# A gated mix of two spectral filters on one core: the order of the first loads, two sums done in halves, rows of half the spectrum, and the last block

## The chip, the core and the metric

One core of a Trainium2 chip runs the whole kernel as one program. The metric is the device time of one execution in microseconds (us); lower is better. Five engines work side by side, each through its own instructions in order: TensorE (matmuls, PE in the profile; the loads of its stationary operand are the rows PEld), VectorE (DVE), ScalarE (ACT), GpSimd (POOL) and SyncE (SP), which here only issues DMA transfers. They wait for each other through semaphores.

## The reference

```python
def _ref(x, w_r, w_i):                       # the same for A and for B
    X = jnp.fft.rfft2(x.astype(jnp.float32), axes=(-2, -1))      # x: 1 x 2048 x 1024
    X = X * (w_r + 1j * w_i)                                      # w: 2048 x 513
    return jnp.fft.irfft2(X, s=(S, D), axes=(-2, -1)).astype(jnp.bfloat16)

x = A_x
g = sigmoid((x * gate_w).sum(-1, keepdims=True))
out = g * _ref(x, A_w_r, A_w_i) + (1 - g) * _ref(x, B_w_r, B_w_i)
```

Both filters act on the same x. So there is one forward transform, two products with weights, and one inverse transform into which the gate is folded.

## The kernel before

The transforms are matmuls with constant tables, in stages. A unit of work fills two of the eight banks of the matmuls' accumulators (PSUM, 1024 columns of float32); there are four such units, and most matmul outputs are copied out by ScalarE, some by VectorE (`act_copy`, `dve_copy`, lines 325 and 328).

- Stage 1 (`stage1`, lines 440 and 447): the first part of the transform over the 2048 rows. x comes in eight blocks `c` of four row groups, 512 KB each; each block is worked for two sets of 128 columns, `j`. `prep` (lines 419 and 423) writes a mirrored copy of the block, or, for the blocks in `FOLDED`, sum and difference, which halve the matmul columns. `mvariant` (lines 412 and 414) scales the table M into three more forms. `evict1` writes the tile FT.
- Stage 2 (`stage2`, line 476) does the transform over the 1024 columns as a sum over `j`, stage 4 (`stage4`, line 491) the rest of the rows. The work is split in two sets of frequencies, M and O, of eight pieces each; two pieces form a group q, four groups to a set. `evict4` leaves a group's spectra in a slot of the tile XR; three slots serve "direct" groups, two serve swapped ones. `swap` (POOL) makes a copy of a group with real and imaginary partitions exchanged by two DMAs.
- Products (`product`, line 521, VectorE): D with the direct spectra, S with the swapped ones, each in two halves of 128 columns; D writes the tile WB, S the tile WA. The weights W lie in WA too: set M needs columns 0 to 384 of a row (`("W", "M", q)`), set O a further 128 (`("W", "O", b)`), which are loaded over columns of M that have been used by then, from 258 on.
- Gate: `gate_weights` (POOL reverses a row at line 526, TensorE multiplies at 528), `gate_spectrum` (line 535), `row_sums` (VectorE, lines 554 and 555, with the table VC), `star_column` and `star_products` (one column of the spectrum, with W's column 256), later `gate_diag`, `zsum`, `sigma`, `gate_sign`.
- Stage 5 (`stage5`, line 575): the inverse over part of the rows, 32 groups g of eight frequencies; groups from 16 up need all products of set M, the others all of set O. `edge` (line 653) forms two columns by themselves for group 0. `evict5` writes the tile WB.
- Stages 6 and 7 (`stage6`, line 675; `stage7`, line 688): for each of 16 blocks r the rest of the inverse. `evict6` and `odd_copy` bring results out, `finals` (line 701, VectorE) adds and subtracts, and SP stores the block. `rbgen` makes the gated tables for stage 6.

The order on each engine is written out by hand in the text `PLAN`: a token is name, arguments, unit, engine (`s2.M.1.1.pe` is stage 2, set M, piece 1, unit 1 on TensorE; `a` is ScalarE, `d` VectorE). An engine's instructions are the tokens for it, from left to right. `Prog` derives the waits from what each instruction reads and writes. Loads are issued in the order of the code ahead of the plan: SP's queue holds x with M's pieces, then F2 and a first part of CK, then W of set M in four groups, two further parts of CK (KI and CL) and, by the plan, W of set O and the tables U5 and DI. Twelve matmuls on zeros (line 375) run while the first loads are under way.

Of the kernel before, what the change touches and what calls it, by code (L numbers as in the profile page):

```python
# [10 lines left out]
HA, HB = 258, 264  # L11
# [139 lines left out]
mv.0.2..d mv.0.1..d mv.0.3..d pp.0..d s1.0.0.0.pe mv.1.1..a mv.2.1..d mv.3.1..d mv.2.3..a mv.2.2..d s1.0.1.1.pe  # L151
e1.0.0..a pp.1..d e1.0.1..a gw.2.pe s1.1.0.3.pe pp.2..d egw..a s1.1.1.0.pe e1.1.0..a s1.2.0.1.pe e1.1.1..d
mv.7.1..a s1.2.1.2.pe mv.4.2..a pp.3..d mv.4.1..a mv.4.3..a e1.2.1..a mv.5.1..d s1.3.1.3.pe pp.4..d e1.2.0..a
mv.6.3..d s1.4.1.0.pe mv.6.2..d mv.7.3..d mv.6.1..d e1.3.1..a s1.3.0.2.pe pp.5..d s1.4.0.1.pe e1.3.0..a pp.6..d
s1.5.0.3.pe e1.4.0..a mv.7.2..d s1.6.0.2.pe e1.4.1..d e1.5.0..a s1.6.1.1.pe pp.7..d e1.6.0..a s1.7.0.0.pe
e1.6.1..d s1.5.1.3.pe e1.7.0..a s1.7.1.2.pe e1.5.1..d e1.7.1..a s2.M.1.1.pe s2.M.0.0.pe e2.M.1..a s2.M.2.3.pe
e2.M.0..a s4.M.1.2.pe e2.M.2..a s4.M.0.1.pe e4.M.1..a s4.M.2.0.pe e4.M.0..a gs.3.3.pe e4.M.2..a D.M.0.0..d
sw.M.0..dma s2.M.3.2.pe egs.3..a D.M.0.1..d s2.M.4.1.pe e2.M.3..a gs.1.0.pe e2.M.4..a s4.M.3.3.pe egs.1..a
s4.M.4.2.pe e4.M.3..a s2.M.5.1.pe e4.M.4..a D.M.1.0..d sw.M.1..dma gs.0.0.pe e2.M.5..a S.M.0.1..d s2.M.7.3.pe
egs.0..a s4.M.5.2.pe S.M.0.0..d e2.M.7..a gs.2.1.pe e4.M.5..a D.M.1.1..d s4.M.7.0.pe egs.2..a sw.M.2..dma  # L160
rows..d s2.M.6.3.pe e4.M.7..a s2.O.1.2.pe e2.M.6..a S.M.1.1..d s2.O.0.1.pe e2.O.1..a D.M.2.0..d s4.M.6.0.pe
e2.O.0..a S.M.1.0..d s4.O.1.3.pe e4.M.6..a wo.0..spq s4.O.0.2.pe D.M.2.1..d e4.O.1..a sw.M.3..dma s2.O.3.1.pe
e4.O.0..a S.M.2.0..d s2.O.2.0.pe e2.O.3..a S.M.2.1..d s2.O.7.3.pe e2.O.2..a D.M.3.0..d s4.O.3.2.pe sw.O.0..dma
e2.O.7..a s4.O.2.1.pe D.M.3.1..d e4.O.3..a s2.O.6.0.pe e4.O.2..a D.O.0.0..d s4.O.7.3.pe e2.O.6..a S.M.3.0..d
s2.O.5.2.pe e4.O.7..a s4.O.6.1.pe S.M.3.1..d e2.O.5..a st.0.pe s2.O.4.3.pe D.O.1.0..d sw.O.1..dma wo.1..spq
e4.O.6..a s5.16.2.pe e2.O.4..a dz.1..d dz.0..d s5.19.1.pe e5.16..a D.O.0.1..d s5.24.3.pe est..a e5.19..a
D.O.3.0..d s4.O.4.2.pe e5.24..a S.O.0.1..d s4.O.5.0.pe e4.O.4..a s5.20.1.pe S.O.0.0..d e4.O.5..a s5.25.3.pe
e5.20..a stp..d sw.O.2..dma D.O.1.1..d s5.17.2.pe e5.25..a s5.23.0.pe S.O.1.0..d e5.17..a s5.21.1.pe D.O.3.1..d
e5.23..a s5.18.3.pe e5.21..a S.O.1.1..d s5.27.2.pe e5.18..a D.O.2.1..d sw.O.3..dma zs.0.0.pe e5.27..a
s5.26.1.pe D.O.2.0..d s5.30.3.pe S.O.2.1..d e5.26..a s5.22.2.pe e5.30..a S.O.2.0..d U5..dma s5.31.1.pe e5.22..a  # L170
# [94 lines left out]
def bass_gated_mix__spectral_gfnet__spectral_gfnet__prompt_kernel(nc, A_x, A_w_r, A_w_i, B_x, B_w_r, B_w_i, gate_w, out):  # L265
# [20 lines left out]
    ATB = sb("ATB", 32)  # L286
    XST = sb("XST", 64)
# [60 lines left out]
    FOLDED = (1, 3, 5)  # L348


    MP = ((0, 4), (4, 16), (16, 32))
# [503 lines left out]
```

## Time and profile before

| What | us |
| --- | --- |
| time, median of 3 runs (lowest to highest) | 128.36 (128.15 to 129.1) |
| the profiled execution's own time | 128.09 |
| its span, first to last instruction | 126.2 |
| stage 1's first matmul / stage 2's first matmul | 7.85 / 23.49 |
| first matmul of stage 5 / its end, by the chain | 53.34 / 91.79 |
| first matmul of stage 6 / last store issued | 92.87 / 123.73 |

| Engine | busy us | share of the span |
| --- | --- | --- |
| PE | 114.4 | 91% |
| PEld | 98.9 | 78% |
| ACT | 103.7 | 82% |
| DVE | 88.4 | 70% |
| POOL | 14.2 | 11% |

Times inside the execution count from the start of the span. In the table by windows, each row is a stretch of the span: its length, then each engine's busy time with the count of its instructions, TensorE's granted clock, the DMA engines' share and their GB/s. In a timeline a row is: start, length, engine, line, operation, output and input, shapes, count; the bracket gives the idle time before it and what ended it. "q" behind an engine's name is its instruction queue, where DMA transfers are issued. In the chain of work that ended last, a row is start, length and what the end waited for there. Matmuls are pipelined: a 128-column matmul is shown 219 ns long but the next starts 56 ns later, so costs of TensorE are taken from start to start.

### The profile page before, as it was taken

What the parts mean: (1) busy time and instruction counts of PE and PEld (TensorE: products, weight loads), DVE (VectorE), ACT (ScalarE), POOL (GpSimd) and SP (SyncE); (2) the same over time, 40 slices, a digit from 0 to 9 for tenths busy, and PEclk for the clock granted to TensorE, in tenths of its full rate; (3) what the DMA queues carried; (4) which work ended last, traced back from release to release, by engine and by line L of the source; (5) the groups of instructions that cost most, each with busy time, mean ns of one, the idle gap of its engine ahead of it and who ended that gap; (6) DMA issues with size and microseconds to landing.
All of it is one profiled execution on the core that took longest, in us unless ns stands there. A gap on an engine that the chain in (4) does not pass through costs nothing.

```text
span 126.2 us, 3590 instructions
## 1 busy us (share of the span) xinstructions
PE 114.4 (91%) x1538; PEld 98.9 (78%) x1538; DVE 88.4 (70%) x120; ACT 103.7 (82%) x124; POOL 14.2 (11%) x31
## 2 busy tenths in 40 slices
PE   6957789699999999999999999999969999999950
PEld 2246569579688695797999989999969999999920
DVE  0075997206198999999999989994001977787782
ACT  0448999598888999999998996998969788988850
POOL 5800000003023033041303000000000000000000
PEclk9999999999999999999999999999999999999999
DMA  2999999999999999979744596000000243443344
GB/s 49 298 346 343 348 374 337 255 272 284 336 303 352 359 322 311 215 192 208 151 166 166 140 405 291 8 0 5 0 0 5 100 173 143 169 168 140 121 160 166
DMA packets 26832, 25.81 MB, mean 205 GB/s; under 512 B 10241, under 2 KB 22801, under 8 KB 26561
## 3 DMA queue, kind: packets, MB, share of 16 engines
q1 hardware_dynamic: 24144, 20.11, 52.3%
q0 software_dynamic: 1584, 4.43, 9.7%
q10 hardware_dynamic: 1088, 1.05, 2.5%
q8 instruction: 12, 0.20, 0.7%
q14 instruction: 4, 0.02, 0.1%
HBM read 17.19 MB, written 4.19 MB: 169 GB/s over the span
## 4 chain that ended last, share of the span: by engine, by line
PE 44%; DVE 23%; DMA 11%; ACT 11%; issue 5%; SPq 3%; DVEq 1%
PE PS L675 11%; DVE WB L521 11%; PE PS L688 11%; DVE WA L521 10%; PE PS L575 10%; DMA XR<-c_M 7%; DMA XR<-XR 5%; ACT FT L325 4%; PE PS L476 4%; ACT WB L325 4%; PE PS L447 3%; PE PS L491 3%; SPq L322 3%; ACT XR L412 1%; ACT WA L325 1%
## 5 line engine op out<-in xcount | busy, mean ns | idle before, releaser
L575 PE MATMUL PS<-CK,WA 128*128 128x128 bf16 x256 | 34.0, 232 | 0.4 <-DVE WA L521 0.3
L575 PEld LDWEIGHTS PS<-CK,WA 128*128 128x128 bf16 x256 | 33.4, 153 | 0.8 <-DVE WA L521 0.6
L575 PE MATMUL PS<-CK,WB 128*128 128x128 bf16 x256 | 33.9, 225 | 0.0
L575 PEld LDWEIGHTS PS<-CK,WB 128*128 128x128 bf16 x256 | 33.5, 153 | 0.4 <-ACT WB L325 0.2
L325 ACT ACTIVATE WB<-PS 128x1024 bf16<-128x1024 f32 (+1 forms) x31 | 31.2, 1022 | 2.3 <-PE PS L575 1.5
L325 ACT ACTIVATE XR<-PS 128x1024 bf16<-128x1024 f32 x32 | 30.0, 1050 | 3.0 <-PE PS L476 2.0
L701 DVE TENSOR_TENSOR WA<-PS,WA 128x512 bf16<-128x512 f32 x32 | 21.4, 725 | 15.8 <-ACT WA L325 15.8
L325 ACT ACTIVATE WA<-PS 128x1024 bf16<-128x1024 f32 (+2 forms) x33 | 25.2, 820 | 5.0 <-PE PS L675 4.8
L521 DVE TENSOR_TENSOR WB<-XR,WA 128x2048 bf16<-128x2048 bf16 x16 | 19.1, 1222 | 9.2 <-PE PS L535 6.6
L521 DVE TENSOR_TENSOR WA<-XR,WA 128x2048 bf16<-128x2048 bf16 x16 | 19.0, 1223 | 0.3 <-DMA XR<-XR 0.3
L476 PE MATMUL PS<-F,FT 128*128 128x128 bf16 x256 | 15.8, 219 | 1.1 <-ACT FT L325 1.1
L688 PE MATMUL PS<-FT,WA 128*128 128x256 bf16 x128 | 16.4, 273 | 0.2 <-ACT WA L325 0.2
L476 PEld LDWEIGHTS PS<-F,FT 128*128 128x128 bf16 x256 | 14.7, 98 | 2.4 <-ACT FT L325 1.4
L491 PE MATMUL PS<-XR,CK 128*128 128x512 bf16 (+1 forms) x72 | 15.3, 355 | 0.0
L675 PE MATMUL PS<-XR,WB 128*128 128x128 bf16 x208 | 13.4, 219 | 1.1 <-ACT WB L325 1.1
L322 POOL DMA_DIRECT2D XR<-XR x16 | 8.4, 528 | 46.9 <-ACT XR L325 35.2
L675 PEld LDWEIGHTS PS<-XR,WB 128*128 128x128 bf16 x208 | 12.5, 98 | 1.5 <-ACT WB L325 1.3
L688 PEld LDWEIGHTS PS<-FT,WA 128*128 128x128 bf16 x128 | 11.9, 98 | 1.6 <-ACT WA L325 0.5
L325 ACT ACTIVATE FT<-PS 128x1024 bf16<-128x1024 f32 x12 | 11.5, 1025 | 1.8 <-PE PS L447 1.6
L447 PE MATMUL PS<-XR,WB 128*128 128x256 bf16 x40 | 9.1, 273 | 1.7 <-DVE XR L414 1.4
L491 PEld LDWEIGHTS PS<-XR,CK 128*128 128x128 bf16 x72 | 6.6, 98 | 4.9
L447 PE MATMUL PS<-XR 128*128 128x256 bf16 x40 | 9.1, 272 | 0.0
(65 smaller groups left out, 92.5 us busy)
## 6 DMA issues: line engine op xcount, KB each, us to landing
XR<-XR POOLq DMA_DIRECT2D x16, 256.0 KB, 4.0
out_dram<-WA SPq DMA_DIRECT2D x16, 256.0 KB, 2.0
WB<-in_A_x_dram SPq DMA_DIRECT2D x12, 256.0 KB, 8.2
FT<-c_U SPq DMA_DIRECT2D x2, 1024.0 KB, 7.0
WA<-in_A_w_r_dram SPq DMA_DIRECT2D x7, 192.5 KB, 4.2
WA<-in_A_w_i_dram SPq DMA_DIRECT2D x7, 192.5 KB, 4.5
WA<-in_B_w_r_dram SPq DMA_DIRECT2D x7, 192.5 KB, 5.3
WA<-in_B_w_i_dram SPq DMA_DIRECT2D x7, 192.5 KB, 5.4
```

The source lines that it names most:

```text
L322: return P.add(eng, lambda e: e.dma_start(dst, src), dma=name, **kw)
L325: return P.add("act", lambda e: e.activation(dst, src, ACT.Copy), **kw)
L412: P.add("act", lambda e: e.activation(o, i, ACT.Copy, scale=sc), **kw)
L447: P.add("pe", lambda e, o=o, lh=lh, rh=rh, s=s: e.matmul(o, lh, rh, start=(s == 0), stop=(s == 1)), r=[("x", c)] + mk + ([("zone", z)] if ...
L476: P.add("pe", lambda e, o=o, lh=fblock(cmb, j, t), j=j, rh=rh: e.matmul(o, lh, rh, start=(j == 0), stop=(j == 1)), r=["F1", "F2"], w=[("ps ...
L491: P.add("pe", lambda e, o=o, fb=FB[kind, pm, m], m=m, rh=rh: e.matmul(o, sl(CK, fb, [(1, 128)]), rh, start=(m == 0), stop=(m == 1)), r=["C ...
L521: pop[st, q, sw, half] = P.add("dve", lambda e: e.tensor_tensor(out=o, in0=x, in1=w, op=ALU.mult), r=xr(o_, 2048) + wk, a=[("prod", st, sw ...
L575: P.add("pe", lambda e, o=o, lh=sl(t, to + l0, [(hp, 128)]), ab=ab: e.matmul(o, lh, KI(ab), start=(ab == 0), stop=(ab == 1)), r=[("prod", ...
L675: P.add("pe", lambda e, o=o, lh=lh, rh=rh, cp=cp: e.matmul(o, lh, rh, start=(cp == 0), stop=(cp == 1)), r=["Z", ("RB", r)], w=[("ps", 2 * ...
L688: P.add("pe", lambda e, o=o, lh=lh, rh=rh, ri=ri: e.matmul(o, lh, rh, start=(ri == 0), stop=(ri == 1)), r=[("Y", r), "DI"], w=[("ps", 2 * ...
L701: P.add("dve", lambda e, s=s, op=op: e.tensor_tensor(out=sl(WA, oo + 512 * s, [(1, 2), (2, 256)]), in0=ps(2 * u * 512, [(256, 2), (1, 256) ...
```

## The change

It has these parts.

- Loads. M's first piece (now four pieces instead of three) goes to SP ahead of x, its second to ACT; the small table SM goes to ACT's queue first. Of x, seven blocks come as before, half from SP and, for the first four, half from ACT; block 7 comes by columns, six smaller transfers on SP, so that `j` = 0 has a load of its own. The gate's small loads on POOL wait for block 5. The tables VC and MK move from POOL to SP, behind W of set M.
- Stage 1: folded blocks are 5 and 6 instead of 1, 3 and 5; the two passes of a unit run one after the other; 11 zero matmuls at the start instead of 12, and 6 and 2 more of them ahead of two units. Block 7 is copied and evicted in halves.
- Stage 2 on the first two pieces is split: the part with `j` = 0 first, then that with `j` = 1.
- Half rows in WA have 257 columns instead of 258. W's column 256 is copied out (four `dve_copy` into WQ) before W of set O is written over it.
- Stage 5's groups 2 and 3 take the even and the odd frequencies of 16; stage 6 on blocks 0 and 1 is split in even and odd, and the even part needs only the groups without odd ones. `edge` does some matmuls for two columns at once.
- The last block's four results go to two banks, its additions and subtractions are done in four pieces instead of two, and its store is split between SP and ACT.
- A new `PLAN` orders all of it. The gate's weights move from stage 1 to behind the third swap, the row sums behind the products of group 2.

```diff
-HA, HB = 258, 264
+HA, HB = 257, 264
-    FOLDED = (1, 3, 5)
-    MP = ((0, 4), (4, 16), (16, 32))
+    FOLDED = (5, 6)
+    MP = ((0, 4), (4, 8), (8, 16), (16, 32))
...
+    def xcols(c, j, eng):
+        for dh in range(2):
+            for lo, n in ((0, 128), (384, 128)) if j == 0 else ((128, 256),):
+                src = AP(x2.tensor, x2.offset + 4 * c * 1024 + 512 * dh + lo, [[32 * 1024, 64], [1024, 4], [1, n]])
+                dma(eng, f"x{c}{j}", sl(WB, 2048 * c + lo, [(512, 4), (1, n)], p0=dh, np_=64, pstep=2), src, a=[("x", c, j)])
...
-    for _ in range(12):
+    for _ in range(11):
...
-    mload(0, "pool")
-    dma("pool", "SM", SM[:], cst_sm.ap(), w=["SM"])
-    for c in range(8):
+    dma("act", "SM", SM[:], cst_sm.ap(), w=["SM"])
+    mload(0, "sp")
+    for c in range(7):
         xload(c, 0, "sp")
         xload(c, 1, "act" if c < 4 else "sp")
-        if c in (0, 3):
-            mload(1 + c // 3, "sp")
+        if c == 0:
+            mload(1, "act")
+        if c in (1, 3):
+            mload((3, 2, 0, 3)[c], "sp")
+    for j in range(2):
+        xcols(7, j, "sp")
...
-    dma("pool", "VC", VC[:].bitcast(u16), cst["V"].ap(), w=["VC"])
-    dma("pool", "MK", MK[:].bitcast(u16), cst["MK"].ap(), w=["MK"])
...
+    dma("sp", "VC", VC[:].bitcast(u16), cst["V"].ap(), w=["VC"])
+    dma("sp", "MK", MK[:].bitcast(u16), cst["MK"].ap(), w=["MK"])
     dma("sp", "KI", sl(CK, 1024, [(1, 256)]).bitcast(u16), cst["CK"].ap()[:, 1024:1280], w=["KI"])
...
+    IDLE = {(1, 0): 6, (2, 0): 2}
...
+        for _ in range(IDLE.get((c, j), 0)):
+            P.add("pe", lambda e: e.matmul(ps(u * 1024, [(1, 512)]), sl(F2, 0, [(1, 128)]), sl(F2, 0, [(1, 512)]), start=True, stop=True),
+                  r=["F2"], w=[("ps", 2 * u)])
...
-    def stage2(st, i, u):
+    def stage2(st, i, u, js=(0, 1)):
...
-        w = sl(WA, WN + row * RA + ((257 if st == "M" else 258) if half else lo), [(2 * RA, 8), (RA, 2), (1, 128)])
+        w = sl(WA, WN + row * RA + ((257 if st == "M" else 256) if half else lo), [(2 * RA, 8), (RA, 2), (1, 128)])
...
+        if st == "M" and half and not sw:
+            dve_copy(sl(WQ, row, [(1, 16)]), sl(WA, WN + row * RA + 256, [(RA, 16)]), r=wk, a=[("W", "O", q // 2, "go"), "WQ"])
...
+    LASTP = 2
+    def cols5(g):
+        return (8 * LASTP + g - LASTP, 2) if g in (LASTP, LASTP + 1) else (8 * g, 1)
...
-    def stage6(r, u):
+    def stage6(r, u, pis=(0, 1)):
...
-                          r=["Z", ("RB", r)], w=[("ps", 2 * u + b // 2)])
+                          r=[("Z", pi), ("RB", r)], w=[("ps", 2 * u + b // 2)])
...
+        for p0, n in ((0, 1), (1, 1)) if r == LASTR else ((0, 2),):
...
+        for s, eng in ((0, "sp"), (1, "act")) if r == LASTR else ((None, "sp"),):
```

The plan from stage 2's start to stage 5's start, and around stage 6's start, as the change has it:

```diff
+s2a.M.1.0.pe e1.7.1.1..d
+e1.7.1.0..a s2a.M.0.1.pe s2b.M.1..pe s2b.M.0..pe e2.M.1..a s2.M.3.2.pe e2.M.0..a s4.M.1.3.pe e2.M.3..a
+s4.M.0.0.pe e4.M.1..d s2.M.2.1.pe e4.M.0..a s2.M.4.2.pe e2.M.2..a D.M.0.0..d sw.M.0..dma s4.M.3.3.pe e2.M.4..a
+D.M.0.1..d s4.M.2.0.pe e4.M.3..a s4.M.4.1.pe e4.M.2..a s2.M.6.2.pe e4.M.4..a sw.M.1..dma D.M.1.0..d s2.M.5.3.pe
+e2.M.6..a s2.O.0.0.pe D.M.1.1..d e2.M.5..a s4.M.6.1.pe e2.O.0..a S.M.0.0..d s4.M.5.2.pe e4.M.6..a S.M.0.1..d
+s2.M.7.3.pe e4.M.5..a s4.O.0.0.pe e2.M.7..a sw.M.2..dma gw.1.pe s2.O.1.2.pe S.M.1.1..d egw..a e4.O.0..a
+s4.M.7.3.pe S.M.1.0..d e2.O.1..a gs.0.1.pe D.M.2.0..d e4.M.7..a s4.O.1.0.pe egs.0..a gs.1.2.pe sw.M.3..dma
+D.M.2.1..d e4.O.1..a wo.0..spq gs.3.3.pe egs.1..a D.O.0.0..d s2.O.3.1.pe egs.3..a S.M.2.0..d gs.2.0.pe
+e2.O.3..a s2.O.2.2.pe S.M.2.1..d egs.2..a st.3.pe e2.O.2..a s4.O.3.1.pe rows..d sw.O.0..dma s2.O.4.0.pe est..a
+e4.O.3..a D.M.3.1..d s2.O.5.2.pe e2.O.4..a D.M.3.0..d s4.O.2.3.pe e2.O.5..a s2.O.6.1.pe S.M.3.1..d e4.O.2..a
+s4.O.4.0.pe e2.O.6..a S.M.3.0..d wo.1..spq s4.O.5.2.pe e4.O.4..a D.O.1.0..d sw.O.1..dma s5.17.3.pe e4.O.5..a
...
+rb.8..d s5.2.2.pe rb.1..d e5.10..a rb.4..d s5.7.3.pe e5.2..a s5.5.0.pe e5.7..a s5.8.1.pe e5.5..a s5.3.2.pe
+e5.8..a e5.3..a s6a.0.3.pe s6a.1.0.pe s6b.1..pe s6.2.1.pe e6.1..a s6.3.2.pe e6.2..a s7.1.0.pe e6.3..a s6b.0..pe
```

More of the change, by code (lines that the diff above doesn't have):

```diff
@@ L156 @@
[L156 to L170, printed above, removed]
@@ new lines, in stage1 @@
+        for s, q in [(s, q) for s in range(2) for q in range(4)] if c not in FOLDED else []:
+            r = 4 * c + q
+            lh = sl(XR, 8192 + 1024 * z + 256 * q + 128 * j, [(1, 128)]) if s else sl(WB, r * 512 + 128 * j, [(1, 128)])
+            rh = sl(XR, 64 * r, [(4096 * s, 2), (2048, 2), (1, 64)])
+            P.add("pe", lambda e, o=ps(u * 1024 + q * 256, [(1, 256)]), lh=lh, rh=rh, s=s, q=q: e.matmul(o, lh, rh, start=(s == 0 and q % 2 == 0), stop=(s == 1), skip_group_check=True),
+                  r=xk(c, j) + mk + ([("zone", z)] if s else []), w=[("ps", 2 * u + q // 2)])
@@ L449, in stage1, with evict1 @@
         zones.drop(c, 2)
-    def evict1(eng, c, j, u):
-        copy(eng, sl(FT, j * 2048 + 4 * c, [(4096, 4), (32, 64), (1, 4)]), ps(u * 1024, [(64, 4), (1, 64), (256, 4)]), r=banks(u), a=["F1"])
+    def evict1(eng, c, j, u, half=None):
+        o, n = (2 * half, 2) if half is not None else (0, 4)
+        copy(eng, sl(FT, j * 2048 + 4 * c + o, [(4096, 4), (32, 64), (1, n)]), ps(u * 1024 + 256 * o, [(64, 4), (1, 64), (256, n)]),
+             r=banks(u)[o // 2:(o + n) // 2], a=[("F1", j)])
     s1end = []
@@ new lines, in edge @@
+        for k, nk, nm, T, se, sm in steps:
+            t, o, st = src[nm]
+            g = [(64, nk)] if nk > 1 else []
+            gi = [(st // 2, nk)] if nk > 1 else []
+            for n, (oo, od, tc, io, idm) in enumerate((
+                    (0, [(1, 64)], TO[T, 0, se], 0, [(st, 64)]),
+                    (4, [(4, 15), (2, 2), (1, 2)], TO[T, 1, sm], 6, [(4 * st, 15), (-2 * st, 2), (st, 2)]),
+                    (0, [(1, 2)], TO[T, 2, sm], 0, [(st, 2)]),
+                    (2, [(1, 2)], TO[T, 1, sm], 2, [(st, 2)]))):
+                for h in range(nk if len(od) == 3 else 1):
+                    gd, ih = (g, gi) if len(od) < 3 else ([], [])
+                    P.add("pe", lambda e, oo=oo + 64 * (k + h), od=gd + od, tc=tc, rh=sl(t, o + io * st + h * (st // 2), ih + idm), g=g, n=n: e.matmul(
+                        ps(u * 1024 + oo, od), sl(CK, tc, [(1, 128)]), rh, start=(bool(g) and n == 0), stop=(not g and n == 3), skip_group_check=True),
+                        r=["CL", "PST", ("prod", "O", 0), ("prod", "O", 1)], w=[("ps", 2 * u)])
```

162 lines of the change are left out of this document (81 added, 81 removed).

## The prediction

> **What bounds the kernel now.** I read the busy table by windows first, one window for each stage.
>
> ```profile
> core 0: us, PE busy (x) PEld busy (x) DVE busy (x) ACT busy (x) POOL busy (x), PEclk, DMA share, GB/s
> ...
> 14.00:23.50 9.50, 7.65 (x81) 6.29 (x81) 7.44 (x15) 8.93 (x11) 0.00 (x0) 1.00 1.08 347
> 23.50:34.00 10.50, 10.50 (x170) 8.52 (x171) 2.38 (x2) 8.55 (x11) 1.06 (x2) 1.00 0.96 282
> 34.00:53.30 19.30, 19.30 (x289) 15.43 (x288) 18.64 (x18) 18.46 (x23) 4.17 (x8) 1.00 1.06 314
> 53.30:73.40 20.10, 19.72 (x274) 18.17 (x272) 20.10 (x21) 19.31 (x21) 4.21 (x8) 1.00 0.67 180
> ```
>
> From 23.5 us on TensorE has no hole: only fewer matmuls, or an earlier start, can shorten it. But from 34 us VectorE is as full, and the DMA engines are full to 53 us. An earlier TensorE helps only as far as these two follow. So next came the VectorE and SP timelines.
>
> ```profile
> 29.38 2.38 DVE L521 TENSOR_TENSOR WB<-XR,WA 128x2048 bf16<-128x2048 bf16 x2 [6.61 <-PE PS L535]
> 34.30 1.23 DVE L521 TENSOR_TENSOR WB<-XR,WA 128x2048 bf16<-128x2048 bf16 x1 [2.55 <-ACT XR L325]
> ...
> 38.94 0.69 DVE L554 TENSOR_TENSOR VT<-VC,GSB 128x512 f32<-128x512 bf16 x1
> ...
> 51.22 2.38 DVE L521 TENSOR_TENSOR WA<-XR,WA 128x2048 bf16<-128x2048 bf16 x2
> ```
>
> ```profile
> 13.51 0.61 SPq L322 DMA_DIRECT2D WA<-in_A_w_r_dram  x1
> ...
> 21.21 1.47 SPq L322 DMA_DIRECT2D WA<-in_B_w_i_dram  x1
> ...
> 27.34 0.62 SPq L322 DMA_DIRECT2D WA<-in_B_w_i_dram  x1
> ...
> 40.02 0.67 SPq L322 DMA_DIRECT2D WA<-in_B_w_i_dram  x1
> 40.73 1.16 SPq L322 DMA_DIRECT2D CK<-c_CK  x2
> ```
>
> The products (L521) multiply spectra by weights W. Group 1 of W has its last load issued at 27.34; the DMA view of that moment gives 4.7 us to landing: 32.0. Its first product starts at 34.30, released by ScalarE. Likewise the last load of group 3 (40.02, 6.1 us) lands at 46.1, and its product runs at 47.72. So the weights had about 2 us in hand. The M products end at 53.60, stage 5's second matmul starts at 53.65, stage 5 ends at 91.79: 38.14 us without a hole.
>
> **The front: 2.5 us earlier.** Stage 2 now starts at 23.49, after a wait of 1.12 for the last eviction. After the change three limits stand close. TensorE: 11 zero matmuls at 0.43 from 1.19 end at 5.9; six unfolded blocks at 2 x 0.87 (16 x 0.109), two folded at 2 x 0.45 and 8 zero matmuls of 512 columns at 0.22 make 14.0: 19.9. x: the last half of block 7 was issued at 11.0 and landed 7.8 later, 18.8; 0.15 MB of small loads ahead of it go (0.4 us at 347 GB/s), while six pieces in place of two give that back; with copy and matmuls (1.1) 19.9. ScalarE: 13 evictions at 0.93 (6.48 for 7) and three scalings at 0.43 from about 7: 20.4, then one half eviction: 21.0. I take 21.0; the half eviction of block 7 lies beside the matmuls on the first 128 columns, so nothing waits there. Bounds: 20.4 (no wait at all) and 22.5.
>
> **What it collides with: the weights come later.** SP issues 14 transfers before F2 now, 19 after: M's first piece and four more parts of x; M's other pieces only change places or go to ACT. Each costs 0.62 to 0.70 with its gap, so SP comes to W 5 x 0.70 = 3.5 us later. Beyond 0.62, the rows between 5 and 23 us hold stalls of 0.40, 0.63, 0.59, 0.39 and 0.85 (21.21 is one), 2.9 in all; nothing shows their cause. If all go, the delay is 0.4; if one more comes, 4.0. Stalls go on in W's rows at about one in seven, so some stay: I take 2.2. From 22.7 to 27.3 loads land 3.3 to 3.8 after issue and SP sets the pace, so a late issue is a late landing; TensorE's earlier start brings none forward.
>
> VectorE in order: D.M.1.0 at 32.0 + 2.2 = 34.2, where its spectra would be there at 30.2. Four products at 1.14 (start to start) and a 16-column copy (0.15; the 32-column cast took 0.18) end S.M.0.1 at 38.9. This frees the slot for swap 2 on POOL (1.05 for two issues), and **behind that swap POOL now has the gate's reversal copy** (0.29), for which TensorE's two gate matmuls wait, to 40.3. TensorE reaches them after nine s2 (0.895) and eight s4 (0.87) at 36.0: a new wait of 4.3 us. All other TensorE work stands behind it.
>
> VC moves from POOL, 4.63, to SP behind W's last load. At 46.1 + 2.2, and 0.5 for its own issue, it lands at 48.8. VectorE reaches the row sums at 48.3: D.O.0.0 needs spectra that are evicted 4.6 after the gate matmuls, 44.9, and it and two more products come first. So the sums start at 48.8, take 1.6 (38.94 to 40.57), and four M products stand behind them: 4 x 1.14 + 0.15, done at **55.1**. TensorE arrives at 40.3 + 14.25 = 54.5. Stage 5 thus starts 1.45 later than at 53.65: the earlier front is eaten, as its cover, TensorE work while weights fly, is used up.
>
> **From there to the end.** TensorE has s2.O.7, s4.O.6 and s4.O.7 left (2.63), 32 groups at 1.0545 (33.74), the gate sums (0.86) and the edges: 26 matmuls for 32 that took 1.57, so 1.28. Sum 38.5, against 38.14: +0.36. O products: VectorE needs 15 x 1.14 and 2.35, 19.5, while TensorE has 16 M groups and the left-overs, 20.4: hidden, with 0.9 in hand; the O weights, 1.1 later still for VC and MK, fit to within 0.7.
>
> The seam before stage 6:
>
> ```profile
> 90.76 1.02 ACT WB L325
> 91.78 0.01 issue
> 91.79 1.03 ACT WB L325
> 92.82 0.05 issue
> 92.87 2.85 PE PS L675 x48
> ```
>
> TensorE sits 1.06 behind the last eviction. The even halves of two stage-6 blocks, 16 matmuls at 0.056 = 0.9, now run there: -0.9, at least 0 if ScalarE is one eviction behind. Last block: four subtractions and additions of 256 columns instead of two of 512 (0.64 start to start). The cost is between 1.28 and 2.56; by columns plus a fixed 0.1 it is 1.5: +0.2, less 0.1 for a store of half the size. Bounds -0.3 and +1.3, +0.1 taken.
>
> **Half rows of 257.** Half of the M products already read W from an odd column (257), and the 32 products span 1.214 to 1.244 us, so I take 0; the far bound is the rate of the casts out of PSUM (L328, 1024 elements in 1.14), which would double a product. [...] The weight loads of stage 5 at pitches of 258 and 264 take the same 153 ns, so 0; were they like L675's (98), matmuls would follow at 0.056 instead of 0.066, and 256 of them would save 2.6.
>
> **Sum** against the profiled execution, 128.09 (span 126.2, 1.9 around it; the median of the runs is 128.36, 0.27 above): 1.45 + 0.36 - 0.9 + 0.1 = +1.0, **129.1**. A measurement tells about 1% (1.28) from no change, so this is "no change, rather slower". Its own range, with the delay between 1.3 and 3.1: 128.2 to 130.0.
>
> **Rivals.**
> 1. *The weights are not late (faster).* With a delay of 0.4 the sum gives -0.8, 127.3. If the queue is also emptier, so that loads land 3.5 after issue as at 23 us and not 4.7 to 6.1, group 1 is there at 31.2, the gate matmuls run at 37.4, D.O.0.0 at 42.0, and 3.4, 1.6 and 4.7 behind it the M products end at 51.7: -2.4, 125.7. Together 126.6. For it: the stalls are unexplained. Against it: the 0.62 of each issue is not a stall, and latency rises just when the swaps start, which now start earlier.
> 2. *Full delay (slower).* With 4.0, stage 5 starts at 56.9: +2.8, 130.9. It decides from a delay of 2.5, where the sum passes 1%.
> 3. *The wait makes TensorE slow.* At the start 12 matmuls of 512 columns take 5.30 us, 0.43 apart, from 1.19 to about 5.9; later 512 columns take 0.22 (L491). The granted clock reads 1.00 in both. The longest hole while it ran fast is 1.4 us; a hole of 4.3 is not in the trace. If it throws TensorE back for another 4.7 us, 2.3 us of work are late, of which 0.6 hide before the M products: +1.7 on the forecast, 130.8, or 132.6 on rival 2. [...]
> 4. *Half rows matter.* Cheaper weight loads, -2.6: 126.5. Dearer products: 20 lie before stage 5, and each 0.1 us on one is 2 us on the sum, 131.1. The even rows above speak against both.
>
> **Chances.** Forecast 0.40, rival 1 0.27, rival 2 0.17, rival 3 0.11, rival 4 0.05. Faster by over 1%: most of rival 1 and half of 4, 0.24. Within 1%: 0.36, from the forecast and the rest of 1. Slower: 0.40, from 2, 3 and the upper end of the forecast. The range leaves out the lower end of rival 1 and the sums of 2 and 3: 126.0 to 131.6.
>
> **What would show it.** Right: the first W load is issued near 15.7; stage 2 starts at 21; TensorE idles some 4 us before the gate matmuls, released by POOL; VectorE's row sums wait for VC; stage 5 starts near 55; no idle time before stage 6. Wrong: D.M.1.0 starts by 32 and TensorE has no hole between 21 and 53 (rival 1); matmuls of 512 columns 0.43 apart after the hole (rival 3); products off 1.22, or weight loads off 153 ns (rival 4).

## The result, and the profile after

| | us |
| --- | --- |
| predicted (range) | 129.1 (126.0 to 131.6) |
| after, median of 4 runs (lowest to highest) | 139.6 (139.09 to 140.16) |
| before, run beside it | 128.25 |
| ratio, with its 95% interval | 1.0879 (1.0803 to 1.0954) |
| the profiled execution after / its span | 140.16 / 138.4 |

The change makes the kernel 8.8% slower, far outside the range. Where the 12.2 us of span come from is seen by cutting both spans at the same two matmuls; for stage 5 the second matmul is taken, as in the prediction.

| Stretch | before | after | difference |
| --- | --- | --- | --- |
| start to stage 2 | 23.49 | 36.30 | +12.8 |
| stage 2 to stage 5 | 30.16 | 31.28 | +1.1 |
| stage 5 to the end of the span | 72.55 | 70.82 | -1.7 |

So the front, which was to be 2.5 earlier, is 12.8 later, and the end, which was to be 0.4 shorter, is 1.7 shorter. The list of waits of after names the front's cause in one row: engine, line, releaser, and then the us in total, the count and the longest.

```profile
PE PS L451 <- DMA F<-c_F: 12.6, 1, 12.6
```

Line 451 is the zero matmuls ahead of two units of stage 1. They waited 12.6 us for a DMA, and the DMA is the load of F2. TensorE's timeline of after shows what stands behind them:

```profile
7.17 0.60 PE L467 MATMUL PS<-XR 128*128 128x256 bf16 x4
20.36 2.74 PE L451 MATMUL PS<-F 128*128 128x512 bf16 x6 [12.59 <-DMA F<-c_F]
...
36.30 2.85 PE L498 MATMUL PS<-F,FT 128*128 128x128 bf16 x48 [0.29 <-ACT FT L327]
...
53.09 0.19 PE L552 MATMUL PS<-GR 128*128 128x8 bf16 x2 [1.62 <-issue]
...
67.58 0.27 PE L606 MATMUL PS<-CK,WA 128*128 128x128 bf16 x1 [0.19 <-DVE WA L543]
```

The first two units of stage 1 end near 7.7. Then TensorE stands until 20.36. The chain of work that ended last follows this back to SP's queue and forward to stage 2:

```profile
15.24 5.07 DMA F<-c_F
20.31 0.04 issue
20.36 2.74 PE PS L451 x6
...
27.39 8.86 ACT FT L327 x10
```

F2 is set to zero at the start, and the 11 matmuls at the start read it. But the code that issues F2's load stands ahead of the plan, and so ahead of stage 1. A matmul in stage 1 that reads F2 is, in the order of the code, a reader of the loaded table. It waits for the load, and it multiplies the table, not zeros (its result is overwritten either way). The load is the 20th transfer of SP's queue, issued at 15.24.

The windows of after show a second cost of the hole. PEclk is the granted clock.

```profile
core 0: us, PE busy (x) PEld busy (x) DVE busy (x) ACT busy (x) POOL busy (x), PEclk, DMA share, GB/s
7.70:20.30 12.60, 0.07 (x1) 0.00 (x0) 3.65 (x15) 2.46 (x5) 1.76 (x3) 0.66 1.11 344
20.30:36.30 16.00, 15.27 (x121) 11.21 (x121) 5.44 (x9) 10.96 (x13) 0.00 (x0) 0.84 0.96 257
...
46.80:67.30 20.50, 18.88 (x312) 14.62 (x309) 17.88 (x21) 17.05 (x24) 4.87 (x10) 1.00 0.55 157
```

The clock is down in the hole (0.66 on its mean) and behind it (0.50 from 20.36 to 23.10), and the six matmuls at 20.36 come 0.43 apart, as at the start of the program. After that, the chain goes through ten evictions of ScalarE in a row (8.86 us) to stage 2. The stretch from 46.8 is the one that was full before: here the DMA engines are at 0.55 of their share, since the weights had 13 us more time. For that reason after itself says little on the rest of the prediction: the hole covers what was to be late. The experiments take the hole away first.

### The profile page after: what moved, and what is told of

Its sections match the earlier page's. It is cut to its first block, busy times and chain, and to the rows that moved or that the text cites. A ratio compares the mean times of both kernels' runs of the same rounds, so it can differ in the third digit from the quotient of the medians.

```text
span 138.4 us, 3605 instructions
## 1 busy us (share of the span) xinstructions
PE 116.6 (84%) x1539; PEld 98.4 (71%) x1539; DVE 87.2 (63%) x129; ACT 104.0 (75%) x125; POOL 12.2 (9%) x27
## 4 chain that ended last, share of the span: by engine, by line
PE 42%; DVE 20%; ACT 17%; SPq 10%; issue 4%; DMA 4%; DVEq 0%; ACTq 0%
SPq L324 10%; DVE WA L543 10%; PE PS L724 9%; PE PS L706 9%; ACT WB L327 8%; PE PS L498 7%; ACT FT L327 6%; PE PS L513 6%; DVE WB L543 6%; PE PS L606 5%; DMA F<-c_F 4%; PE PS L467 3%; PE PS L451 2%; ACT WA L327 2%; DVE WA L740 2%
## 5 line engine op out<-in xcount | busy, mean ns | idle before, releaser
L606 PE MATMUL PS<-CK,WA 128*128 128x128 bf16 x256 | 31.9, 224 | 0.3 <-DVE WA L543 0.2
L606 PEld LDWEIGHTS PS<-CK,WA 128*128 128x128 bf16 x256 | 31.2, 145 | 1.1 <-DVE WA L543 0.9
L606 PE MATMUL PS<-CK,WB 128*128 128x128 bf16 x256 | 32.0, 225 | 0.0
L606 PEld LDWEIGHTS PS<-CK,WB 128*128 128x128 bf16 x256 | 31.3, 145 | 0.5
L327 ACT ACTIVATE XR<-PS 128x1024 bf16<-128x1024 f32 x31 | 29.3, 1056 | 2.5 <-PE PS L498 1.5
L740 DVE TENSOR_TENSOR WA<-PS,WA 128x512 bf16<-128x512 f32 (+1 forms) x34 | 21.6, 694 | 14.1 <-ACT WA L327 14.0
L327 ACT ACTIVATE FT<-PS 128x1024 bf16<-128x1024 f32 (+1 forms) x15 | 13.3, 1005 | 12.2 <-PE PS L467 12.2
L498 PE MATMUL PS<-F,FT 128*128 128x128 bf16 x256 | 15.9, 219 | 0.3 <-ACT FT L327 0.3
L498 PEld LDWEIGHTS PS<-F,FT 128*128 128x128 bf16 x256 | 14.8, 98 | 1.5 <-ACT FT L327 0.6
L451 PE MATMUL PS<-F 128*128 128x512 bf16 x8 | 3.3, 568 | 12.6 <-DMA F<-c_F 12.6
L724 PEld LDWEIGHTS PS<-FT,WA 128*128 128x128 bf16 x128 | 11.8, 98 | 2.0 <-ACT WA L327 0.9
L706 PEld LDWEIGHTS PS<-XR,WB 128*128 128x128 bf16 x208 | 12.5, 98 | 1.0 <-ACT WB L327 0.7
L451 PEld LDWEIGHTS PS<-F 128*128 128x128 bf16 x8 | 0.9, 129 | 14.0 <-DMA F<-c_F 12.9
```

The costliest lines, as they stand in the source:

```text
L327: return P.add("act", lambda e: e.activation(dst, src, ACT.Copy), **kw)
L451: P.add("pe", lambda e: e.matmul(ps(u * 1024, [(1, 512)]), sl(F2, 0, [(1, 128)]), sl(F2, 0, [(1, 512)]), start=True, stop=True), r=["F2"], ...
L498: P.add("pe", lambda e, o=o, lh=fblock(cmb, j, t), j=j, rh=rh, cmb=cmb: e.matmul(o, lh, rh, start=(j == 0 and cmb == 0), stop=(j == 1), sk ...
L606: P.add("pe", lambda e, o=o, lh=sl(t, to + l0, [(hp, 128)]), ab=ab: e.matmul(o, lh, KI(ab), start=(ab == 0), stop=(ab == 1)), r=[("prod", ...
L706: P.add("pe", lambda e, o=o, lh=lh, rh=rh, cp=cp: e.matmul(o, lh, rh, start=(cp == 0), stop=(cp == 1)), r=[("Z", pi), ("RB", r)], w=[("ps" ...
L724: P.add("pe", lambda e, o=o, lh=lh, rh=rh, ri=ri: e.matmul(o, lh, rh, start=(ri == 0), stop=(ri == 1)), r=[("Y", r), "DI"], w=[("ps", bank)])
```

## The experiments

Ratios are to the kernel before, run beside each kernel on the same chip, with 95% intervals.

**Is it the wait for F2?** Two kernels that still have the wait, with one execution each, and two that don't.

```diff
-    IDLE = {(1, 0): 6, (2, 0): 2}
+    IDLE = {(1, 0): 1}
```

> The changed kernel with one matmul of the 8 kept, the first, still reading F2. Theory A: it waits for the load as eight do, TensorE stands still from 7.7 to about 20.3, and only the matmuls' own time goes: 136.5 to 138.5. Rival, the loss grows with their number: under 130.

Measured: 138.38. One matmul instead of eight saves 1.2 us, not the 10 or so that a loss growing with their number would give: it waits 11.8 us for the same load. So the work of the matmuls is not the cost.

The second puts the same eight matmuls, and nothing else of the change, into stage 1 of the kernel before.

> The kernel before with the same 8 matmuls put into its stage 1, 6 ahead of block 1's first unit and 2 ahead of block 2's, reading F2; nothing else. F2 was issued at 12.33 and landed 7.7 us later, at 20.0, where block 1 now begins at 10.65. Theory A: TensorE stands still until 20.0, then 6 matmuls at 0.43, so stage 2 begins 10 to 12 us later, at 33.5 to 36, and the time is 137 to 140. Rival, the wait hurts only with the new order: under 131.

Measured: 139.77. The waits of this kernel:

```profile
PE PS L434 <- DMA F<-c_F: 8.5, 1, 8.5
```

F2's load is earlier there, and the wait is 8.5 us, but the kernel ends as late as after. This one part is enough for a loss of that size.

Now without them:

```diff
-    IDLE = {(1, 0): 6, (2, 0): 2}
+    IDLE = {}
```

> The changed kernel without the 8 matmuls inside stage 1 (IDLE is empty); the 11 at the start stay. Theory A, the wait for F2's load is the loss and nothing else changed: stage 2 begins near 21 instead of 36.3, but the weights (group 1 landed at 34.0 in the changed kernel) and the gate's copy on POOL then stand in the way, stage 5 begins at 54 to 55, and from there it takes the 70.8 us that the changed kernel takes (67.6 to 138.4): span 125 to 126, time 127.2, between 126 and 128.2. Rival B, no second wait behind the first: stage 5 begins near 51, time 123 to 124. Rival C, x by columns or the new order of loads is the loss too: stage 2 begins after 25, time over 130.

And with the eight matmuls on zeros that nothing overwrites, as the word "zero" promises:

```diff
+    P.add("dve", lambda e: e.memset(sl(XR, 12288, [(1, 512)]), 0.0), w=["ZT"])
...
-            P.add("pe", lambda e: e.matmul(ps(u * 1024, [(1, 512)]), sl(F2, 0, [(1, 128)]), sl(F2, 0, [(1, 512)]), start=True, stop=True),
-                  r=["F2"], w=[("ps", 2 * u)])
+            P.add("pe", lambda e: e.matmul(ps(u * 1024, [(1, 512)]), sl(XR, 12288, [(1, 128)]), sl(XR, 12288, [(1, 512)]), start=True, stop=True),
+                  r=["ZT"], w=[("ps", 2 * u)])
```

> The changed kernel, its 8 matmuls in stage 1 kept, but reading 512 zeros of their own (written by VectorE at the start into a part of XR that stage 1 does not use) instead of the tile F2, whose load they wait for. Theory A: within 1 us of the kernel without them, about 127.2 or up to 0.5 less if TensorE then runs at full rate in more of stage 1; no wait of over 2 us in stage 1. Rival, the 8 matmuls themselves or the clock are the loss: near 139.

Measured: 131.77, ratio 1.0204 (1.0143 to 1.0264), and 131.87, ratio 1.0223 (1.0172 to 1.0275). The wait for F2 is gone, and 8 us with it. Whether the matmuls are there or not makes no difference that can be measured. The second is within 1 us of the first, as expected, but both lie over 3 us above the 127.2 that was expected: a kernel without the wait is still 2% slower than before. Stage 2 starts at 22.98 and 23.15, only 0.5 and 0.3 earlier than before, and there is a new hole. POOL's timeline of the kernel without the matmuls, and its list of waits:

```profile
40.37 1.04 POOL L324 DMA_DIRECT2D XR<-XR  x2 [6.71 <-DVE WA L543]
41.41 1.06 POOL L550 COPY GR<-GR 128x128 bf16<-128x128 bf16 x1
```

```profile
PE PS L552 <- issue: 4.4, 1, 4.4
```

The gate matmuls (L552) run at 42.57, right after the reversal copy on POOL, which stands behind swap 2, which waits for VectorE's products. (The list names no engine for this wait, but the copy ends at 42.47.) This is the wait that the prediction put at 4.3. Windows of one us show what follows it: the granted clock is 0.50 from 41.0 to 47.8 in this kernel, and from 42.6 to 46.0 in the other, whose hole is 4.0. In the latter the next four matmuls of 512 columns come 0.43 apart, the sign that the prediction had named for its rival 3.

**The wait, the clock, and the late weights.** The reversal copy only needs the gate's own load. This kernel is the one on own zeros, with the copy as a token of its own, `gr`, ahead of the swaps:

```diff
-s4.M.0.0.pe e4.M.1..d s2.M.2.1.pe e4.M.0..a s2.M.4.2.pe e2.M.2..a D.M.0.0..d sw.M.0..dma s4.M.3.3.pe e2.M.4..a
+s4.M.0.0.pe e4.M.1..d s2.M.2.1.pe e4.M.0..a s2.M.4.2.pe e2.M.2..a D.M.0.0..d gr..p sw.M.0..dma s4.M.3.3.pe e2.M.4..a
```

> The changed kernel with zeros of its own for the 8 matmuls, and the gate's reversal copy on POOL put ahead of the first swap instead of behind the third. Theory A, the second wait (4.0 us before the gate matmuls, released by POOL) and the half rate after it are what is left of the loss, and then the weights bind: no hole before the gate matmuls, granted clock 1.00 from 34 us on, M products done near 54 instead of 58.3, time about 127.5, between 126.5 and 128.5. Rival, the weights of group 1 (VectorE's wait until 34.8) set the end by themselves: time still over 130.

The next leaves the copy late, but fills the hole with 18 matmuls of 512 columns on F2's table, which has long been loaded by then, so that the clock stays up:

```diff
         P.add("pool", lambda e: e.tensor_copy(sl(GR, 128, [(1, 128)]), sl(GR, 127, [(-1, 128)])), r=["GR"], w=["GRr"])
+        for _ in range(18):
+            P.add("pe", lambda e: e.matmul(ps(u * 1024, [(1, 512)]), sl(F2, 0, [(1, 128)]), sl(F2, 0, [(1, 512)]), start=True, stop=True),
+                  r=["F2"], w=[("ps", 2 * u)])
```

> The changed kernel with zeros of its own, the reversal copy left behind the third swap, and 18 matmuls of 512 columns (3.9 us) put ahead of the gate matmuls, whose results are overwritten: the wait stays, TensorE is busy in it. If the hole throws TensorE to half rate, the 6.6 us after it become 5.1, granted clock 1.00, M products done 1.5 earlier, time near 130.3 against 131.9 without the fill. If the hole costs only its length, no change, 131.9 or slightly more.

Measured: 130.69, ratio 1.0212 (1.0158 to 1.0266), and 130.92, ratio 1.0223 (1.0188 to 1.0257). The first misses its theory's range and is where its rival had it, over 130. With the copy early the hole is gone, and the gate matmuls run at 38.36, 4 us sooner, but little of this arrives at the end. VectorE's timeline of that kernel shows the next limits:

```profile
34.91 2.38 DVE L544 TENSOR_TENSOR WB<-XR,WA 128x2048 bf16<-128x2048 bf16 x2 [3.38 <-DMA WA<-in_B_w_i_dram]
...
47.51 2.38 DVE L544 TENSOR_TENSOR WA<-XR,WA 128x2048 bf16<-128x2048 bf16 x2 [1.93 <-DMA XR<-XR]
50.06 0.69 DVE L581 TENSOR_TENSOR VT<-VC,GSB 128x512 f32<-128x512 bf16 x1 [0.17 <-DMA VC<-c_V]
```

The weights hold the products until 34.91, for 3.38, and a swapped group's transfer until 47.51, for 1.93. VC, late from SP's queue, is the last thing on the chain before the row sums at 50.06, but holds VectorE only 0.17 more. Stage 5's second matmul waits 2.01 for the products and starts at 56.40. So there were two late things side by side, the copy and the weights, and each covers part of the other. The granted clock takes its share too. Stage 5 starts 1.9 earlier than on own zeros alone (58.33), but in this execution the clock falls to 0.50 from 57.5 to 60.9, soon after the hole of 2.01, and from stage 5 to the end it takes 72.3 instead of 70.8: 1.5 of the 1.9 are lost there.

With the hole filled, the granted clock is 1.00 from the start to 124 us, and from the gate matmuls to stage 5 it takes 14.5 us (43.86 to 58.35) instead of 16.0 (42.31 to 58.33) on own zeros and 16.65 without the matmuls. The lowered clock thus costs 1.5 to 2.2 us there. The gain did not reach the end: the ratio is the 1.0223 of the kernel without the fill. In the profiled execution the weights of group 1 were 1.5 later (VectorE waits for them until 36.31, not 34.81), and stage 5 starts at the same time; whether this is so in the other executions is not shown.

Then both repairs together: the early copy, and block 7 of x in two loads instead of six.

```diff
-    for j in range(2):
-        xcols(7, j, "sp")
+    for dh in range(2):
+        src = AP(x2.tensor, x2.offset + 4 * 7 * 1024 + 512 * dh, [[32 * 1024, 64], [1024, 4], [1, 512]])
+        dma("sp", "x7", sl(WB, 2048 * 7, [(512, 4), (1, 512)], p0=dh, np_=64, pstep=2), src, a=[("x", 7, 0), ("x", 7, 1)])
```

> As the kernel with the early copy, and block 7 of x again by two transfers on SP instead of six. Theory A, SP's issues set when the weights land: four issues fewer, group 1's first product 2 to 3 us earlier than 34.8, M products done near 52, time 125.0 to 126.3. Rival, the transfers and not the issues are the limit, or TensorE's own work binds first: same as the kernel with the early copy within 0.5.

And the same edit alone, with the copy left behind swap 2:

> The changed kernel, zero matmuls on zeros of their own, block 7 of x by two loads instead of six; the gate's reversal copy stays behind swap 2. Theory (the late weights cause the wait at the gate matmuls, and both losses come from SP's extra issues): the first W load is issued near 12.9 instead of 15.9, D.M.1.0 starts near 32.5 instead of 34.8, swap 2 follows 2.3 us earlier, and the idle time before the gate matmuls falls from 4.0 to 1.3 to 1.9 us, too short to lower the granted clock: 127.3 to 128.6. Rival (the copy's place behind the swap costs what it costs, whenever the weights come): the wait stays above 3.5 us, TensorE runs at half rate after it, 130 to 131.

Measured: 127.48, ratio 0.9951 (0.9921 to 0.998), and 128.70, ratio 1.0049 (1.0007 to 1.009). Together with the two kernels above this makes a square:

| ratio to before | six loads of block 7 | two loads |
| --- | --- | --- |
| copy behind swap 2 | 1.0223 | 1.0049 |
| copy ahead of the swaps | 1.0212 | 0.9951 |

Four fewer issues on SP, with the holes and falls of the clock that hang on them, are worth 1.7 to 2.6%, and the early copy is worth 1% once the weights are in time, and nothing before. The two rows of SP's queue at the first W load show the size: without the four issues it goes out at 12.88, with them at 15.92.

```profile
15.92 0.61 SPq L324 DMA_DIRECT2D WA<-in_A_w_r_dram  x1
```

```profile
12.88 0.61 SPq L324 DMA_DIRECT2D WA<-in_A_w_r_dram  x1
```

(The first is of the kernel with the early copy alone, the second of the one with both.) D.M.1.0 then starts at 32.56, released by ScalarE and not by a load. This is the 2.3 us that was expected, but the time, 127.48, is above the theory's 125.0 to 126.3: the M products are done near 54 and not 52. VectorE's timeline of the kernel with both repairs shows a later limit, the transfer of a swapped group, and stage 5's second matmul still waits 1.20 for the products:

```profile
39.35 2.38 DVE L545 TENSOR_TENSOR WA<-XR,WA 128x2048 bf16<-128x2048 bf16 x2 [2.04 <-DMA XR<-XR]
```

With block 7 alone the hole before the gate matmuls shrinks from 4.0 to 2.12, where 1.3 to 1.9 was expected, and the time is just above its range; the clock stays at 1.00. The gate matmuls run at 40.88 instead of 42.31, so the late weights, by way of D.M.1.0 and swap 2, had caused about a third of that wait; the other 0.45 is TensorE, which reaches them later in that execution.

**The parts at the end.** The half rows of 257 alone, in the kernel before:

```diff
-HA, HB = 258, 264
+HA, HB = 257, 264
```

(with the copies of column 256 into WQ and set O's halves at column 256, as in the change)

> The kernel before with half rows of 257 alone (W's column 256 copied out first). Theory, the pitch of WA makes stage 5's weight loads shorter: 145 ns instead of 153 and a matmul every 0.0605 us instead of 0.0659, 2.7 us less on TensorE; ScalarE needs about 1.02 a group against 0.97 then, so 0.5 to 2 us of it reach the end: 126.5 to 128. Rival, the loads are shorter because of the new order of stage 5: 153 ns again, time as before or up to 0.6 slower for four small copies on VectorE.

Measured: 127.09, ratio 0.9914 (0.9874 to 0.9954). The groups of stage 5's weight loads, before first; after the bar are busy us and mean ns of one:

```profile
L575 PEld LDWEIGHTS PS<-CK,WB 128*128 128x128 bf16 x256 | 33.5, 153 | 0.4 <-ACT WB L325 0.2
L575 PEld LDWEIGHTS PS<-CK,WA 128*128 128x128 bf16 x256 | 33.4, 153 | 0.8 <-DVE WA L521 0.6
```

```profile
L578 PEld LDWEIGHTS PS<-CK,WB 128*128 128x128 bf16 x256 | 31.4, 145 | 0.5 <-ACT WB L326 0.2
L578 PEld LDWEIGHTS PS<-CK,WA 128*128 128x128 bf16 x256 | 31.2, 145 | 2.2 <-DVE WA L522 2.0
```

The only tile whose pitch changed is WA, from 258 to 257 columns; WB's stays 264. Both groups fall from 153 to 145 ns. A stretch of 191 matmuls on the chain of both kernels shows what TensorE gains, 0.066 and 0.062 from one matmul to the next:

```profile
73.36 12.58 PE PS L575 x191
```

```profile
73.16 11.81 PE PS L578 x191
```

From stage 5's second matmul to the end of the span it is 71.31 us instead of 72.55.

The reverse, in the kernel with both repairs: the pitch back to 258.

> The third repair (127.48) with the pitch of the M products' half rows back at 258 columns, all else as in it. Theory (odd pitch makes stage 5's weight loads cheaper, 145 for 153 ns, and its matmuls 0.0605 apart for 0.0659; ScalarE's evictions at 1.02 keep part of the 2.6 us away): weight loads back at 153 ns for both tiles, 1.05 us for each group on TensorE, 128.3 to 129.0. Rival (the weight loads differ, but ScalarE's evictions set the pace of stage 5 in this kernel anyway): 127.3 to 127.8.

Measured: 128.77, ratio 1.0081 (1.0042 to 1.0121), against 0.9951. The weight loads are back:

```profile
L610 PEld LDWEIGHTS PS<-CK,WB 128*128 128x128 bf16 x256 | 33.2, 152 | 0.5
L610 PEld LDWEIGHTS PS<-CK,WA 128*128 128x128 bf16 x256 | 33.2, 152 | 0.8 <-DVE WA L545 0.5
```

Stage 5 starts at 54.30, as in the kernel with both repairs (54.17), and from there to the end it is 72.4 instead of 70.83. So the odd pitch is worth 1.2 us in the one kernel and 1.6 in the other, all of it in stage 5. (In this execution the granted clock was 0.50 from 43.9 to 47.3, ahead of stage 5; two others, with a mean of 1.00, took 128.60 and 128.94, so the clock isn't what makes the kernel longer.)

The parity seam, on top of the half rows in the kernel before (groups 12 and 13 hold the even and odd columns, 13 comes last):

```diff
-e5.6..a s5.12.3.pe e5.0..a e5.12..a s6.0.2.pe s6.1.1.pe e6.0..a s6.2.0.pe
+e5.6..a s5.13.3.pe e5.0..a e5.13..a s6a.0.2.pe s6a.1.1.pe s6b.0..pe e6.0..a s6b.1..pe s6.2.0.pe
```

> The kernel before with half rows of 257 (127.09) and, on top, the parity seam alone: groups 12 and 13 of stage 5 hold even and odd columns, group 13 is the last, and the even halves of the first two stage-6 blocks run before its eviction has ended. The idle time before stage 6 was 1.12 us with half rows of 257; 16 matmuls at 0.056 fit into it. Theory (the seam is worth what the prediction took, 0.9, less what the order of two more evictions takes back): 126.1 to 126.5. Rival (ScalarE's evictions are the bound there, and what TensorE saves it waits for later): 126.9 to 127.3.

Measured: 126.67, ratio 0.9897 (0.9855 to 0.9938): the fastest kernel of the study. Against half rows alone, the difference between the two ratios (0.0017, some 0.2 us) lies within their intervals, and 126.67 lies between the two expected ranges, so the times don't settle it. One profile of each shows what happens: TensorE's timeline at the seam of this kernel has

```profile
90.61 1.07 PE L685 MATMUL PS<-XR,WB 128*128 128x128 bf16 x16 [0.19 <-ACT WB L326]
...
91.83 1.96 PE L685 MATMUL PS<-XR,WB 128*128 128x128 bf16 x32 [0.15 <-ACT WB L326]
```

The 1.12 us of idle time became two of 0.19 and 0.15, and the even halves run in between. But ScalarE's last four evictions take 3.90 us by the chain instead of 3.61, so the last one ends 0.28 later, and 70.81 us from stage 5 to the end against 71.31 leaves 0.5 of the 0.9.

The seam undone in the kernel with both repairs:

```diff
-e5.8..a e5.3..a s6a.0.3.pe s6a.1.0.pe s6b.1..pe s6.2.1.pe e6.1..a s6.3.2.pe e6.2..a s7.1.0.pe e6.3..a s6b.0..pe
+e5.8..a e5.3..a s6.0.3.pe s6.1.0.pe s6.2.1.pe e6.1..a s6.3.2.pe e6.2..a s7.1.0.pe e6.3..a
```

> The third repair (own zeros, early reversal copy, block 7 by two loads; 127.48) with the parity seam undone: stage 6 begins both blocks after the last eviction of stage 5. Theory (seam worth 0.9): stage 6's 16 matmuls from 91.2 move behind the eviction's end at 92.3, 128.2 to 128.5. Rival (ScalarE sets the end of stage 5 and the order after it, the seam is worth under 0.3): 127.4 to 127.8.

Measured: 129.01, ratio 1.0062 (1.0021 to 1.0103), 1.1% above the kernel with the seam and more than either theory said. Its profiled execution is one of its longer ones (129.72), with the clock lowered early in stage 5 (0.83 on the mean of 54 to 64, matmuls 0.107 apart from 55.4 on instead of 0.061) after an idle time of 1.89, which has nothing to do with the seam; so only the seam itself is read from it: idle times of 0.29 and 0.90 before stage 6, where the kernel with the seam has one of 0.27. From stage 5 to the end this execution takes 73.2, 2.4 more than with the seam; a fall of the clock as long as this one cost 1.5 in the kernel with the early copy alone, which leaves 0.9, an estimate, for the seam. Nor does the clock make the 1.1% (0.5 to 1.6%): the five executions with a mean granted clock of 0.991 or more take 127.55 to 129.23, with 128.85 in the middle, and the four such of the kernel with the seam 126.80 to 127.62. That the seam saves idle time is shown; why undoing it costs more than 0.9 in the times stays open.

The kernel with both repairs (0.9951) is no faster than the kernel before with half rows alone (0.9914) or with half rows and seam (0.9897). So nothing here shows a gain from the rest of the change, the new loads and the new order.

## Why the prediction was wrong

**The step that failed** is in the part on the front: "two folded at 2 x 0.45 and 8 zero matmuls of 512 columns at 0.22 make 14.0". The eight matmuls are a term of work there, 1.8 us. They were taken for the same kind as the eleven at the start, since both read F2 and both are called zero matmuls. The question that the prediction asks of VC and of the reversal copy, what does this instruction wait for, was not asked of them. Everything for the answer was at hand: `r=["F2"]` in the diff, the place of F2's load in SP's queue, which the prediction itself moves ("SP issues 14 transfers before F2 now, 19 after"), and its landing time. By these numbers: F2 was issued at 12.33 and took 7.7 to land before, so 20.0; five issues at 0.70 later it is issued at 15.8, and with the 3.3 to 7.8 that the prediction gives for loads to land it is there between 19 and 24. Measured: 15.24, and 20.3. The row of before:

```profile
12.33 0.67 SPq L322 DMA_DIRECT2D F<-c_F  x1
```

A unit of stage 1 that was to run at about 8 could thus not run before 20. The kernels with and without the wait show that this alone is the 8 us between 139.6 and 131.8. The term was put at 1.8 us of work, and what the runs show in its place is a wait of 12.6.

The other steps, read where the hole doesn't cover them:

- **"The front: 2.5 us earlier": wrong too.** Without the wait, stage 2 starts at 22.98 to 23.60, from 0.5 earlier to 0.1 later. Even this is no gain: the two kernels of the experiments that keep the front of before start it at 22.75 and 22.79. The bound that failed is ScalarE's, "13 evictions at 0.93 ... and three scalings at 0.43 from about 7". ScalarE does start near 7, but after two evictions and two more scalings it stands until the last of M's pieces has come, because the scaling of that piece is next in its order. Its timeline in the kernel with both repairs, and then rows of the chain there:

```profile
12.07 0.51 ACT L426 ACTIVATE XR<-XR,SM 128x256 bf16<-128x256 bf16 x1 [2.05 <-DMA XR<-c_M]
12.49 11.16 ACT L327 ACTIVATE FT<-PS 128x1024 bf16<-128x1024 f32 x13
```

```profile
4.55 7.49 DMA XR<-c_M
...
12.58 10.56 ACT FT L327 x12
```

  Eleven evictions and two halves of block 7 (the row names only the larger shape) run from 12.5 and end at 23.6, and stage 2's first half, at 23.19, needs all but the last half. The evictions were counted right, but the wait for M between the second and the third was put at nothing. In the kernel before, the same load stood on the chain, with the same scaling behind it, and the prediction did not use these rows:

```profile
4.27 8.49 DMA XR<-c_M
12.78 1.71 ACT XR L412 x4
```

- **"The weights come later": right.** SP's timeline of after:

```profile
16.34 0.61 SPq L324 DMA_DIRECT2D WA<-in_A_w_r_dram  x1
...
28.79 0.62 SPq L324 DMA_DIRECT2D WA<-in_B_w_i_dram  x1
```

  First W load predicted at 15.7, measured 15.9 to 16.3 in the kernels with six loads. Group 1's last load was to be 2.2 later than 32.0, 34.2; in after it lands at 34.0, and D.M.1.0 starts at 34.8 to 36.3 in the four kernels with six loads and without the wait for F2. What six loads cost against two is the square's 1.7 to 2.6%, 2.2 to 3.3 us.
- **"A new wait of 4.3 us" at the gate matmuls: right**, 4.4 and 4.0, released by POOL. In after it is 1.62, since by then the weights had landed. The copy's length was not right: 0.29 was its time alone; right behind a swap's issues it took 1.00 to 1.06.
- **"VectorE's row sums wait for VC": seen** in the kernel with the early copy alone (50.06, predicted 48.8), but as a wait of 0.17, and not in the others, where something else was later.
- **Rival 3, the clock: its mechanism is real.** Holes of 4.0 and 4.4 lowered the granted clock to 0.50 for 3.4 and 6.8 us, and 1.5 to 2.2 us were lost, where the rival priced 1.7. The prediction had given this 0.11, because no hole of this length was in the trace of before; the wait that makes the hole, however, was in its own forecast. The fall began 2.9 us after the start of the longer hole and 4.3 after the start of the shorter one, just behind its end; other falls, below, followed shorter holes or none.
- **131.8 and the rivals' 132.6** (full delay and slow clock together) lie close by chance: the delay was not the full 4.0, as the first W load was 2.4 to 2.8 later. Against the forecast, the profiled kernel without the matmuls runs its gate matmuls 2.3 later (42.57 for 40.3), takes 1.85 more from there to stage 5 (16.65 for 14.8, the clock) and 1.2 less to the end (70.9 for 72.1, the half rows): 2.9 in all, 130.1 for a span of 127.2.
- **Half rows of 257, taken at 0: wrong**, -1.2 to -1.6. The far bound named there, cheaper weight loads, was the case, at 145 ns and not 98. The products stayed at 1.22 to 1.23, so the products' rival fell. The argument "pitches of 258 and 264 take the same 153" compared two even pitches and said nothing on an odd one.
- **Seam -0.9.** The chain of after at the seam:

```profile
94.56 11.12 ACT WB L327 x11
...
105.73 2.41 PE PS L706 x40
```

  The even halves run at 104.52, before these 40 matmuls, and the idle time goes as the prediction said; but ScalarE is the bound here with 11 evictions in a row, and where the seam was added by itself 0.5 of the 0.9 stayed.
- **Last block +0.1:** from TensorE's last matmul to the end of the span it is 4.35 after and 4.47 before, so -0.1.

From stage 5 to the end, the sum of the last three was +0.36 - 0.9 + 0.1 = -0.44, and after has -1.7; the half rows, -1.2 to -1.6, are enough for the difference. The +0.36 was not tried by itself.

## What to carry to other kernels

An instruction that is there to keep an engine busy has operands, and so it has waits: ask of each added instruction what last wrote what it reads, in the order of the code, before giving it a price; a filler is free only if its operands are written once, early. When a late load and a late copy stand side by side, taking one away can show little until the other is gone too, so test them in a square. And on a queue where each transfer costs 0.65 us to issue, cutting a load into more pieces moves everything behind it, here by 3.0 us for four pieces.

## What the runs showed of the hardware that was not expected

- The time shown for stage 5's weight loads went with the distance between the columns of one of the two tiles that they load, for both tiles alike: 153 ns at 258 and 264 elements (516 and 528 bytes), 145 ns for both when only the one goes to 257 (514 bytes), and 152 again when it goes back. Stage 6's loads, whose columns are 2 elements apart, show 98 ns. Stage 5's loads alternate between the tiles; why the unchanged one follows was not tried.
- The granted clock fell after holes of 2.01 and 1.89, and in two kernels without any. The kernel with the early copy alone, by windows of one us:

```profile
43.00:44.00 1.00, 1.00 (x39) 1.00 (x36) 1.00 (x2) 0.50 (x2) 0.67 (x2) 0.93 1.05 352
44.00:45.00 1.00, 1.00 (x12) 1.00 (x11) 1.00 (x3) 0.18 (x1) 0.00 (x0) 0.50 1.10 380
...
58.00:59.00 1.00, 1.00 (x12) 1.00 (x11) 1.00 (x2) 0.59 (x1) 0.00 (x0) 0.50 0.86 120
```

  By the shares, the clock falls at 43.9 and again at 57.5. The second fall follows a hole of 2.01 that ended at 56.40. The first follows no hole; but 96 of the matmuls from 40.17 to 43.84 have 3 columns each. The same order of matmuls in the kernel with both repairs kept 1.00, as did the kernel with block 7 alone, with a hole of 2.12. The kernel with both repairs and pitch 258 fell at the same place as the one with the early copy alone. The hole of 1.89 is that of the kernel without the seam, so a hole's length alone doesn't tell what the clock does, and the expectation that called holes of 1.3 to 1.9 too short to lower it, which no run had shown for 1.9, was wrong there. Whether the few columns have a part in the first fall was not tried; it stays open.
- POOL's copy of 128 x 128 took 0.29 us alone and 1.00 to 1.06 right behind the issues of a swap.
